# The last two result blocks of a decode layer: other widths, one summed in the bank of the chunks, and their copies and stores on other engines

## The chip, the cores and the metric

The kernel runs on one core of one Trainium2 chip. The metric is the time of one execution on the device in microseconds, the median of several runs. All data are fp32.

## The reference

One transformer layer is computed for eight sequences with one new token each (model width 1024).

```
h   = x + attention(layernorm(x))      # 32 query heads, 4 key/value heads of 128,
                                       # the last 1024 of 4096 cached positions
g   = layernorm(h) @ w_gate            # 1024 x 3584
u   = layernorm(h) @ w_up              # 1024 x 3584
out = h + (gelu(g) * u) @ w_down       # 3584 x 1024
```

The 3584 rows of `w_down` are 28 chunks of 128 rows. The result `out` is a sum over the 28 chunks plus `h`.

## The kernel before, in words

Each weight and each cached key or value is used once per run for only eight tokens. The host lays all of them out as one list of parts in the order of use, and SyncE issues one DMA for each part into two large buffers (`wbuf`). A part is issued when TensorE has finished with the buffer's former content. Most of TensorE's work stands in a loop over stages: eight transposes, then four groups of sixteen products with 512 columns each.

The change lies behind that loop, in the last part of `decode_block`. Chunks 0 to 23 of `w_down` are done in the loop; their sum, with `h`, is gathered by VectorE in `d0`. The activations for all chunks stand transposed in `at`. The 1024 result columns are computed as four groups (NQ = 4) of QW = 256 columns, group j in partitions 32j to 32j + 31, so "column" below means one of these 256.

Chunks 24 to 26 come in parts of two chunks and one (`wd0`, `wd1`), and the function `add` adds their products, and `d0`, in one PSUM bank, `acc`, over 256 columns. ScalarE copies that sum to `s_sb` in SBUF (line 462).

The last chunk, 27, is cut by column into two parts, `we0` and `we1`, whose widths stand in `ENDS`. For each of them TensorE computes four products into a bank of its own (`yt` and `tp`, line 468), VectorE adds `s_sb` and writes `o_fin` (line 471), and the block is stored by a DMA: the first from SyncE's queue, the second from ScalarE's (line 83 is the helper that issues them). SyncE then clears the semaphores and waits for both stores.

The order on each engine is the order of the code. `run` gives each instruction waits on counters of other engines; each engine increments one counter. Where an instruction needs two waits, the first stands as an instruction of its own in front of it. The four products of a block carry their waits on the first of them.

Of the kernel before, what the change touches and what calls it, by code (L numbers as in the profile page):

```python
# [8 lines left out]
P = 128  # L9
# [7 lines left out]
NQ = 4  # L17
CP = 32 // B
QW = D // NQ
# [7 lines left out]
LATE = (5, 6, 4)  # L27

PARTS = (8, 8, 4, 4, 2, 1)
ENDS = (160, 96)  # L30
SINGLES_AT, LAST = 24, 27


class Flow:
# [38 lines left out]
    def run(self, engine, make, *waits, mark=True):  # L73
        ins = self.start(engine, make, waits)
        if not mark:
            return None
        self.done[engine] += 1
        ins.then_inc(self.own[engine], 1)
        return self.own[engine], self.done[engine]

    def move(self, name, out, src, *waits, engine="sync"):
        s = self.sem(name)
        self.start(engine, lambda e: e.dma_start(out, src), waits).then_inc(s, 16)  # L83
        return s, 16
# [6 lines left out]
def decode_block(nc, x, flow, tail, outs):  # L91

    fl = Flow(nc)
    run, move, go = fl.run, fl.move, fl.go
    scale = DH ** -0.5

    def sb(name, *shape):
        return nc.alloc_sbuf_tensor(name, list(shape), F32).ap()

    def bank(name, n):  # L100
        return nc.alloc_psum_tensor(name, [P, n], F32).ap()
# [4 lines left out]
    tp, yt, acc = bank("tp", 2 * N), bank("yt", N), bank("acc", N)  # L106
# [12 lines left out]
    def pe(it, step):  # L119
        return steps, 6 * it + 1 + ("t0", "a0", "a1", "t1", "b0", "b1").index(step)  # L120
# [61 lines left out]
    def load(k, *waits):  # L182
# [15 lines left out]
        out=ident, in_=ident, compare_op=ALU.not_equal, fill=1.0, base=0,  # L198
# [9 lines left out]
        out=own, in_=ident.rearrange("p (a b h) -> p b a h", b=HB, h=REP), axis=AX.XY,  # L208
# [5 lines left out]
    def layernorm(src, ready_, name):  # L214

        bn = sb(name + "_bn", 64, 2, 6)
        mv, ve, sd, r0, r1, r2, rs = (
            sb(f"{name}_{n}", 64, k) for n, k in
            (("mv", 2), ("ve", 1), ("sd", 1), ("r0", 1), ("r1", 1), ("r2", 1), ("rs", 1))
        )  # L220
        a = run("vector", lambda e: e.bn_stats(bn[:, 0], src), ready_)
        run("vector", lambda e: e.tensor_copy(bn[0:32, 1], bn[32:64, 0]), a)
        tok = run("vector", lambda e: e.tensor_copy(bn[32:64, 1], bn[0:32, 0]), a)
        tok = run("vector", lambda e: e.bn_aggr(mv, bn), tok)
        tok = run("vector", lambda e: e.tensor_scalar(ve, mv[:, 1:2], EPS, None, op0=ALU.add), tok)
        tok = run("scalar", lambda e: e.activation(sd, ve, AF.Sqrt), tok)  # L226
        tok = run("vector", lambda e: e.reciprocal(r0, sd), tok)
        tok = run("vector", lambda e: e.scalar_tensor_tensor(
            r1, r0, r0, ve, op0=ALU.mult, op1=ALU.mult), tok)
        tok = run("vector", lambda e: e.tensor_scalar(  # L230
            r2, r1, -0.5, 1.5, op0=ALU.mult, op1=ALU.add), tok)
        tok = run("vector", lambda e: e.tensor_mul(rs, r0, r2), tok)
        return run("vector", lambda e: e.tensor_scalar(
            tin[0:64, 0:N], src, mv[:, 0:1], rs, op0=ALU.subtract, op1=ALU.mult), tok, tin_zero)
# [26 lines left out]
    tok = layernorm(xh, x_in, "ln1")  # L261
# [3 lines left out]
    for hf in range(2):  # L265
# [4 lines left out]
        tok = run("scalar", lambda e: e.copy(q_sb, w0), pe(0, ("a0", "b0")[hf]))  # L270
        tok = run("vector", lambda e: e.tensor_add(tin[:, 0:N], w1, q_sb), tok, pe(0, end),  # L271
                  pe(0, ("t0", "t1")[hf]))
        go("vector", turn, 1, tok, *tp_free)
        qt = tp[:, 0:N].rearrange("p (i s k m) -> p s m k i", i=4, s=2, k=2)
        for s in range(2):
            tok = run("vector", lambda e, s=s: e.tensor_scalar(  # L276
                qz[hf].rearrange("p (s b m) -> p s b m", s=2, b=B)[:, s, :, 0:REP].rearrange(
                    "p b (k i) -> p b k i", k=2),
                qt[:, s, 0::CP], scale, None, op0=ALU.mult), moved, zero[hf])
# [8 lines left out]
    for hf in range(2):  # L288
# [4 lines left out]
        tok = run("vector", lambda e: e.tensor_reduce(  # L293
            out=nmax, in_=s_ps, axis=AX.X, op=ALU.max, negate=True), pe(1, ("a1", "b1")[hf]))
# [3 lines left out]
        tok = run("vector", lambda e: e.reciprocal(rtot, tot), p_ok)  # L298
# [15 lines left out]
    for hf in range(2):  # L314
# [3 lines left out]
        tok = run("scalar", lambda e: e.copy(o1, big[hf][:, 0:N]), pe(2, ("a0", "b0")[hf]))  # L318
        tok = run("vector", lambda e: e.tensor_add(o_sb, big[hf][:, N:2 * N], o1), tok,  # L319
                  pe(2, ("a1", "b1")[hf]))  # L320
        o3 = o_sb.rearrange("p (b d) -> p b d", b=HB)
        out = tin[:, 0:DH]
        tok = run("vector", lambda e: e.tensor_scalar(
            out, o3[:, 0], share[:, 0:1], None, op0=ALU.mult), tok, share_ok,
            pe(2, ("t0", "t1")[hf]))
        for b in range(1, HB):
            tok = run("vector", lambda e: e.scalar_tensor_tensor(
                out, o3[:, b], share[:, b:b + 1], out, op0=ALU.mult, op1=ALU.add), tok)
# [3 lines left out]
        for s in range(2):  # L332
            src = tp[:, 64 * s:64 * s + 64].rearrange("p (b h) -> p h b", h=REP)
            tok = run("vector", lambda e: e.tensor_copy(  # L334
                ot[:, s * REP:(s + 1) * REP], src.unsqueeze(3).to_broadcast([P, REP, B, CP])),
                moved)
# [10 lines left out]
    tok = run("scalar", lambda e: e.copy(y0, ya[:, 0]), pe(3, "a0"))  # L347
    a_out = run("vector", lambda e: e.tensor_add(y1, ya[:, 1], y0), tok, pe(3, "a1"))  # L348
    tok = run("vector", lambda e: e.tensor_add(y1[0:64], y1[0:64], xh), a_out)
# [3 lines left out]
    tok = run("vector", lambda e: e.tensor_add(lo, lo, hi), u, v)  # L353
    top = sb("top", 64, N)
    v = run("scalar", lambda e: e.copy(top, yb[64:P, 1]), pe(3, "b1"))
    tok = run("vector", lambda e: e.tensor_add(lo, yb[0:64, 1], lo), tok, pe(3, "b1"))
# [4 lines left out]
    tok = layernorm(h_sb, h_ok, "ln2")  # L361
    go("vector", turn, 1, tok, pe(3, "t1"))
    xt, tok = spread("xt2", pe(4, "t0"), pe(3, "b1"))
    go("vector", turn, 1, tok)

    at = sb("at", P, DF // P, 32)
# [5 lines left out]
    tok = run("scalar", lambda e: e.copy(gs[0], ya[:, 0]), pe(4, "a0"))  # L372
    tok = run("vector", lambda e: e.tensor_add(gs[0], ya[:, 1], gs[0]), tok, pe(4, "a1"))
    go("vector", ready[0], 3, tok)
    g_ok = run("scalar", lambda e: e.activation(ge[0], gs[0], AF.Gelu_apprx_tanh), tok)
    tok = run("vector", lambda e: e.tensor_copy(us[0], yb[:, 0]), pe(4, "b0"))  # L376
    tok = run("vector", lambda e: e.tensor_add(us[0], yb[:, 1], us[0]), tok, pe(4, "b1"))  # L377
    b_free = tok
    tok = run("vector", lambda e: e.tensor_mul(tin[:, 0:N], ge[0], us[0]), tok, g_ok, pe(4, "t1"))
# [24 lines left out]
    tok = run("scalar", lambda e: e.copy(gs[1], ya[:, 0]), pe(5, "a0"))  # L404
    tok = run("vector", lambda e: e.tensor_add(gs[1], ya[:, 1], gs[1]), tok, pe(5, "a1"))  # L405
# [6 lines left out]
    tok = run("vector", lambda e: e.tensor_add(us[1][0:64], yb[0:64, 0], top), v)  # L412
    tok = run("vector", lambda e: e.tensor_mul(tin[0:64, 0:N], ge[1][0:64], us[1][0:64]), tok)  # L413
# [11 lines left out]
    q0, place = SINGLES_AT, 0  # L425
    for k, src in enumerate(tail[:-len(ENDS)]):
        n = src.shape[1] // D
        here = move(f"wd{k}", later[:, place:place + n * D], src, pe(5, "b0"))
# [3 lines left out]
    blocks = []  # L432
    c0 = 0
    for k, (n, src) in enumerate(zip(ENDS, tail[-len(ENDS):])):
        w = later[:, place + NQ * c0:place + NQ * (c0 + n)]
# [4 lines left out]
    tok = run("scalar", lambda e: e.copy(d0, yb[:, 1]), pe(5, "b1"))  # L440
    tok = run("vector", lambda e: e.tensor_add(d0[0:64], d0[0:64], h_sb), tok)
    for k in range(2):
        tok = run("vector", lambda e: e.tensor_add(d0, ya[:, k], d0), tok, pe(6, f"a{k}"))  # L443
# [3 lines left out]
    def add(lhs, rhs, *waits, start=False, stop=False):  # L447
        for j in range(NQ):
            tok = run("tensor", lambda e: e.matmul(
                acc[32 * j:32 * j + 32, 0:QW], lhs(j), rhs(j), start=start, stop=stop),  # L450
                *waits, mark=(stop and j == NQ - 1))
        return tok

    for q in range(SINGLES_AT, LAST):
        if q == LAST - 1:
            add(lambda j: add2[:, j // 2, :], lambda j: d0[:, (j % 2) * QW:(j % 2) * QW + QW],
                d_ok, consts)
        w, here = rows[q]
        tok = add(lambda j: at[:, q, :], lambda j: w[:, j * QW:(j + 1) * QW], here, at_ok[1],
                  start=(q == SINGLES_AT), stop=(q == LAST - 1))  # L460
    s_sb = sb("s_sb", P, QW)
    s_ok = run("scalar", lambda e: e.copy(s_sb, acc[:, 0:QW]), tok)
    o_fin = sb("o_fin", P, QW)
    done = []
    cut = ENDS[0]
    for (c0, n, w, here), d_ps in zip(blocks, (yt, tp)):
        for j in range(NQ):
            tok = run("tensor", lambda e: e.matmul(  # L468
                d_ps[32 * j:32 * j + 32, 0:n], at[:, LAST, :], w[:, j * n:(j + 1) * n],
                start=True, stop=True), here, mark=(j == NQ - 1))  # L470
        done.append(run("vector", lambda e: e.tensor_add(  # L471
            o_fin[:, c0:c0 + n], d_ps[:, 0:n], s_sb[:, c0:c0 + n]), tok, s_ok))

    nc.vector.br_lt(never, 0, on_true="down", on_false="end").branch_hint(back)
    nc.switch_bb("end")
    sent = [move("out0", outs[0], o_fin[:, 0:cut], done[0]),
            move("out1", outs[1], o_fin[:, cut:QW], done[1], engine="scalar")]

    issued = fl.sem("issued")
    nc.scalar.sem_inc(issued, 1)  # L480
# [75 lines left out]
```

## Time and profile before

| | us |
|---|---|
| median of 3 runs (lowest, highest) | 264.25 (264.11, 264.62) |
| the profiled execution, its own time | 264.19 |
| its span, first to last instruction | 262.8 |
| share of the span in which the weights' queue is busy | 98.4% |

The profile is one execution. Times in its rows count from the start of the span. PE is TensorE's products, PEld its weight loads, DVE VectorE, ACT ScalarE, SP SyncE; SPq and ACTq are the issue of a DMA by these engines. A row of the timeline gives the start, the length, the engine, the line, the operation with output and input, the count, and in brackets the idle time before it and what ended that. An fp32 product stands as two records, so a group of four products is "x8". [...]

### The profile page before, as it was taken

The page shows a single profiled execution, that of the slowest core. Times are in us where ns is not written, and L with a number is a line of the kernel's source. Part 1 is how long each engine was busy: PE and PEld are TensorE (multiplying, and loading weights), DVE is VectorE, ACT ScalarE, POOL GpSimd, SP SyncE. Part 2 cuts the span into 40 slices and gives each one's busy share as a digit, 9 for nine tenths or more (in the row PEclk, how much of TensorE's full clock was granted, in tenths as well). Part 3 has the DMA queues.
Part 4 walks back from the last instruction along what each step waited for, and adds up shares of the span by engine and source line. Part 5 has one row for each costly group of instructions (what it writes and reads, how often), then busy time and mean ns, then how long its engine had stood idle before and what let it go on. Part 6 is the DMA issues. An engine that isn't in the chain of part 4 may idle for free. (4 is left out here: it accounts for less than half of the span.)

```text
span 262.8 us, 2313 instructions
## 1 busy us (share of the span) xinstructions
PE 157.1 (60%) x984; PEld 53.1 (20%) x984; DVE 34.5 (13%) x78; ACT 16.6 (6%) x25; POOL 15.8 (6%) x31
## 2 busy tenths in 40 slices
PE   0024955915937726947617918629909609968596
PEld 0021221211221222212102212122302202323122
DVE  0220010010021110040310020640100300031011
ACT  1000000000030020000000000200200000010000
POOL 5020010010000000001020000020000110000100
PEclk9999996895975955986965995956986965997799
DMA  8998997999899799989979997998999799999995
GB/s 319 484 409 389 479 469 329 479 479 449 349 479 479 329 469 479 449 349 479 479 329 469 479 459 339 479 479 359 439 479 459 339 449 429 414 454 409 429 415 213
DMA packets 3200, 111.31 MB, mean 424 GB/s; under 512 B 496, under 2 KB 752, under 8 KB 1024
## 3 DMA queue, kind: packets, MB, share of 16 engines
q1 hardware_dynamic: 3024, 111.23, 98.4%
q10 hardware_dynamic: 176, 0.08, 0.1%
HBM read 111.18 MB, written 0.13 MB: 424 GB/s over the span
## 5 line engine op out<-in xcount | busy, mean ns | idle before, releaser
L146 PE MATMUL big<-w,st 128*32 128x512 f32 x832 | 137.2, 747 | 68.7 <-PEq L127 67.1
L146 PEld LDWEIGHTS big<-w,st 128*32 128x32 f32 x832 | 37.8, 133 | 160.1 <-issue 157.5
L132 PE MATMUL tp<-ident,tin 128*128 128x128 f32 x104 | 17.5, 322 | 34.4 <-PEq L127 34.4
L132 PEld LDWEIGHTS tp<-ident,tin 128*128 128x128 f32 x104 | 14.0, 166 | 44.7 <-issue 44.7
L255 POOL COPY st<-ot 128x256 f32<-128x256 f32 x8 | 2.9, 401 | 75.4 <-DVE ot L334 75.4
L246 POOL COPY st<-xt 128x1024 f32<-128x1024 f32 x2 | 3.0, 1523 | 54.1 <-DVE xt L241 54.1
L293 DVE TENSOR_REDUCE nmax<-big 128x1 f32<-128x1024 f32 x2 | 2.5, 1225 | 29.0 <-PE big L146 29.0
L271 DVE TENSOR_TENSOR tin<-big,q 128x512 f32<-128x512 f32 x2 | 1.4, 692 | 32.7 <-PE big L146 32.7
L319 DVE TENSOR_TENSOR o<-big,o 128x512 f32<-128x512 f32 x2 | 1.4, 692 | 28.6 <-PE big L146 28.6
L281 POOL COPY st<-qz 128x1280 f32<-128x1280 f32 x2 | 2.5, 1254 | 35.5 <-DVE qz L276 35.5
L255 POOL COPY st<-at 128x256 f32<-128x256 f32 x6 | 2.6, 465 | 32.7 <-DVE tin L413 25.1
L270 ACT COPY q<-big 128x512 f32<-128x512 f32 x2 | 1.2, 586 | 36.0 <-PE big L146 36.0
L405 DVE TENSOR_TENSOR gs<-big,gs 128x512 f32<-128x512 f32 x1 | 0.7, 691 | 19.1 <-PE big L146 19.1
L443 DVE TENSOR_TENSOR d<-big,d 128x512 f32<-128x512 f32 x2 | 1.4, 692 | 13.2 <-PE big L146 13.2
L348 DVE TENSOR_TENSOR y<-big,y 128x512 f32<-128x512 f32 x1 | 0.7, 692 | 18.4 <-PE big L146 18.4
L255 POOL COPY st<-xt 128x256 f32<-128x256 f32 x2 | 1.3, 660 | 30.1 <-DVE us L377 30.1
L318 ACT COPY o<-big 128x512 f32<-128x512 f32 x2 | 1.2, 585 | 28.9 <-PE big L146 28.9
L295 ACT ACTIVATE tin<-big,nmax 128x1024 f32<-128x1024 f32 x2 | 2.2, 1114 | 11.9 <-DVE nmax L293 11.9
L295 ACT ACT_TABLE_LOAD x1 | 1.3, 1283 | 25.1 <-DVE nmax L293 25.1
L226 ACT ACT_TABLE_LOAD x2 | 2.6, 1283 | 1.9 <-POOL ident L197 1.9
L404 ACT COPY gs<-big 128x512 f32<-128x512 f32 x1 | 0.6, 585 | 32.3 <-PE big L146 32.3
L376 DVE COPY us<-big 128x512 f32<-128x512 f32 x1 | 0.7, 692 | 13.1 <-PE big L146 13.1
(69 smaller groups left out, 42.2 us busy)
## 6 DMA issues: line engine op xcount, KB each, us to landing
w<-weights SPq DMA_DIRECT2D x3, 4096.0 KB, 22.3
w<-weights SPq DMA_DIRECT2D x2, 2048.0 KB, 23.3
w<-weights SPq DMA_DIRECT2D x1, 1024.0 KB, 23.8
w<-weights SPq DMA_DIRECT2D x1, 512.0 KB, 24.8
w<-weights SPq DMA_DIRECT2D x1, 320.0 KB, 25.1
w<-weights SPq DMA_DIRECT2D x1, 192.0 KB, 25.1
w<-weights SPq DMA_DIRECT2D x11, 26.9
out<-o_fin SPq DMA_DIRECT2D x1, 80.0 KB, 1.7
```

The lines of the kernel that those rows point to most:

```text
L132: ins = t.transpose(tp[:, i * P:(i + 1) * P], tin[:, i * P:(i + 1) * P], ident)
L146: ins = t.matmul(out[32 * j:32 * j + 32, :], st[i][:, s0:s0 + 32], wbuf[i][:, w0:w0 + N], start=(c == 0), stop=(c == 3))
L226: tok = run("scalar", lambda e: e.activation(sd, ve, AF.Sqrt), tok)
L246: fill = run(engine, lambda e: e.tensor_copy(windows(i), half.unsqueeze(2).to_broadcast([P, 2, NQ, 4 * 32])), tok, *clear)
L255: tok = run(engine, lambda e: e.tensor_copy(windows(i)[:, k, 2 * e2:2 * e2 + 2].rearrange("p h (c m) -> p h c m", m=32), s[:, e2].unsqueez ...
L270: tok = run("scalar", lambda e: e.copy(q_sb, w0), pe(0, ("a0", "b0")[hf]))
L271: tok = run("vector", lambda e: e.tensor_add(tin[:, 0:N], w1, q_sb), tok, pe(0, end), pe(0, ("t0", "t1")[hf]))
L281: fill = run("gpsimd", lambda e: e.tensor_copy(st[hf].rearrange("p (k n) -> p k n", k=2), qz[hf].unsqueeze(1).to_broadcast([P, 2, NQ * WIN ...
L293: tok = run("vector", lambda e: e.tensor_reduce(out=nmax, in_=s_ps, axis=AX.X, op=ALU.max, negate=True), pe(1, ("a1", "b1")[hf]))
L295: p_ok = run("scalar", lambda e: e.activation(tin, s_ps, AF.Exp, bias=nmax, accum_out=tot), tok, pe(1, ("t0", "t1")[hf]))
L319: tok = run("vector", lambda e: e.tensor_add(o_sb, big[hf][:, N:2 * N], o1), tok, pe(2, ("a1", "b1")[hf]))
L443: tok = run("vector", lambda e: e.tensor_add(d0, ya[:, k], d0), tok, pe(6, f"a{k}"))
```

## The change

The blocks are 176 and 80 columns wide. The first is no longer computed in a bank of its own: its products are added in `acc`, on top of the chunks' sum, and ScalarE copies the 176 finished columns straight to `o_fin` and stores them from its own queue. Before that VectorE copies the other 80 columns of the sum out of `acc` to `s_sb`, and the first block's products wait for this copy besides their weights. The second block has the bank `yt`, VectorE's addition, and a store from SyncE's queue.

```diff
-ENDS = (160, 96)
+ENDS = (176, 80)
...
-    s_sb = sb("s_sb", P, QW)
-    s_ok = run("scalar", lambda e: e.copy(s_sb, acc[:, 0:QW]), tok)
+    (a0, na, wa, a_here), (b0, nb, wb, b_here) = blocks
+    cut = na
+    s_sb = sb("s_sb", P, nb)
+    s_ok = run("vector", lambda e: e.tensor_copy(s_sb, acc[:, b0:b0 + nb]), tok)
     o_fin = sb("o_fin", P, QW)
-    done = []
-    cut = ENDS[0]
-    for (c0, n, w, here), d_ps in zip(blocks, (yt, tp)):
+
+    def last(out, n, w, start, *waits):
         for j in range(NQ):
             tok = run("tensor", lambda e: e.matmul(
-                d_ps[32 * j:32 * j + 32, 0:n], at[:, LAST, :], w[:, j * n:(j + 1) * n],
-                start=True, stop=True), here, mark=(j == NQ - 1))
-        done.append(run("vector", lambda e: e.tensor_add(
-            o_fin[:, c0:c0 + n], d_ps[:, 0:n], s_sb[:, c0:c0 + n]), tok, s_ok))
+                out[32 * j:32 * j + 32, 0:n], at[:, LAST, :], w[:, j * n:(j + 1) * n],
+                start=start, stop=True, skip_group_check=not start), *waits, mark=(j == NQ - 1))
+        return tok
+
+    done = [run("scalar", lambda e: e.copy(o_fin[:, 0:na], acc[:, 0:na]),
+                last(acc, na, wa, False, s_ok, a_here))]
+    done.append(run("vector", lambda e: e.tensor_add(o_fin[:, b0:b0 + nb], yt[:, 0:nb], s_sb),
+                    last(yt, nb, wb, True, b_here)))
...
-    sent = [move("out0", outs[0], o_fin[:, 0:cut], done[0]),
-            move("out1", outs[1], o_fin[:, cut:QW], done[1], engine="scalar")]
+    sent = [move("out0", outs[0], o_fin[:, 0:cut], done[0], engine="scalar"),
+            move("out1", outs[1], o_fin[:, cut:QW], done[1])]
```

On TensorE, at the end of its program, the order of the products changes as follows (lines with - stand in the kernel before, with + in the changed one; in brackets the counters that an instruction waits for, `wd1`, `we0` and `we1` being the landings of the last three weight parts):

```order
 L449 MATMUL acc<-w,at 32x256 [waits wd1_done]
 L449 MATMUL acc<-w,at 32x256 x3
-L468 MATMUL yt<-w,at 32x160 [waits we0_done]
-L468 MATMUL yt<-w,at 32x160 x3
-L468 MATMUL tp<-w,at 32x96 [waits we1_done]
-L468 MATMUL tp<-w,at 32x96 x3
+L470 MATMUL acc<-w,at 32x176 [waits vector_done,we0_done]
+L470 MATMUL acc<-w,at 32x176 x3
+L470 MATMUL yt<-w,at 32x80 [waits we1_done]
+L470 MATMUL yt<-w,at 32x80 x3
```

The first block's products stand where they stood, write `acc`, and have a wait for VectorE in front of the one for their weights.

On VectorE, at the end of its program, the two additions become a copy and an addition:

```order
 L441 TENSOR_TENSOR d<-d,h_sb 64x512 [waits scalar_done]
 L443 TENSOR_TENSOR d<-big,d 128x512 [waits vector_done,steps_done] x2
-L471 TENSOR_TENSOR o_fin<-yt,s_sb 128x160 [waits tensor_done,scalar_done]
-L471 TENSOR_TENSOR o_fin<-tp,s_sb 128x96 [waits tensor_done]
-L474 COMPARE_AND_BRANCH
+L465 COPY s_sb<-acc 128x80 [waits tensor_done]
+L477 TENSOR_TENSOR o_fin<-yt,s_sb 128x80 [waits tensor_done]
+L480 COMPARE_AND_BRANCH
```

The copy of the sum moved here from ScalarE, and only the second block's addition is left.

On ScalarE, also at the end, the copy and the store are those of the first block:

```order
 L411 COPY top<-big 64x512 [waits steps_done]
 L440 COPY d<-big 128x512 [waits steps_done]
-L462 COPY s_sb<-acc 128x256 [waits tensor_done]
-L83 DMA out<-o_fin 128x96 [waits vector_done]
+L475 COPY o_fin<-acc 128x176 [waits tensor_done]
+L83 DMA out<-o_fin 128x176 [waits scalar_done]
```

The store waits for ScalarE's own copy in place of VectorE's addition.

## Rows read from the trace of the kernel before

**Rows 1.** The page: span, queue share, bytes and mean rate
```profile
span 262.8 us, 2313 instructions
DMA packets 3200, 111.31 MB, mean 424 GB/s; under 512 B 496, under 2 KB 752, under 8 KB 1024
q1 hardware_dynamic: 3024, 111.23, 98.4%
```

**Rows 2.** The chain that ended last, around the end: start, length, what
```profile
234.86 25.11 DMA w<-weights
```

**Rows 3.** The timeline at the end: start, length, engine, line, operation, count, idle before
```profile
257.99 1.07 PE L449 MATMUL acc<-w,at 128*32 128x256 f32 x16 [0.52 <-DMA w<-weights]
259.28 0.64 PE L449 MATMUL acc<-w,at 128*32 128x256 f32 x8
259.98 0.37 ACT L462 COPY s_sb<-acc 128x256 f32<-128x256 f32 x1 [17.93 <-PE acc L449]
260.00 0.48 PE L468 MATMUL yt<-w,at 128*32 128x160 f32 x8
260.46 0.16 PEld L468 LDWEIGHTS tp<-w,at 128*32 128x32 f32 x8 [0.30 <-DMA w<-weights]
260.47 0.37 PE L468 MATMUL tp<-w,at 128*32 128x96 f32 x8
260.62 0.33 DVE L471 TENSOR_TENSOR o_fin<-yt,s_sb 128x160 f32<-128x160 f32 x1 [2.41 <-PE yt L468]
260.91 0.26 DVE L471 TENSOR_TENSOR o_fin<-tp,s_sb 128x96 f32<-128x96 f32 x1
260.98 0.35 SPq L83 DMA_DIRECT2D out<-o_fin  x1
261.20 0.36 ACTq L83 DMA_DIRECT2D out<-o_fin  x1
```

**Rows 4.** SyncE's queue: issue of the last weight transfer (start, length)
```profile
235.33 0.43 SPq L83 DMA_DIRECT2D w<-weights  x1
```

**Rows 5.** DMA issues: source, queue, count, KB of one, us to landing
```profile
w<-weights SPq DMA_DIRECT2D x1, 192.0 KB, 25.1
out<-o_fin SPq DMA_DIRECT2D x1, 80.0 KB, 1.7
out<-o_fin ACTq DMA_DIRECT2D x1, 48.0 KB, 1.6
```

**Rows 6.** Groups by form: line, engine, shapes, count, busy, mean ns of one
```profile
L334 DVE COPY ot<-tp 128x256 f32<-128x256 f32 x4 | 1.5, 420 | 2.6 <-PE tp L132 2.6
L241 DVE COPY xt<-tp 128x128 f32<-128x128 f32 x4 | 1.0, 286 | 4.4 <-PE tp L132 4.4
...
L270 ACT COPY q<-big 128x512 f32<-128x512 f32 x2 | 1.2, 586 | 36.0 <-PE big L146 36.0
```

**Rows 7.** The timeline where VectorE's result releases TensorE
```profile
207.57 0.69 DVE L379 TENSOR_TENSOR tin<-ge,us 128x512 f32<-128x512 f32 x1
208.43 0.53 PEld L132 LDWEIGHTS tp<-ident,tin 128*128 128x128 f32 x5 [2.64 <-issue]
```

**Rows 8.** Windows over the stores: length, PE, PEld, DVE, ACT, POOL, clock, DMA, GB/s
```profile
261.90:262.00 0.10, 0.00 (x0) 0.00 (x0) 0.00 (x0) 0.00 (x0) 0.00 (x0) 1.00 1.01 298
262.30:262.40 0.10, 0.00 (x0) 0.00 (x0) 0.00 (x0) 0.00 (x0) 0.00 (x0) 1.00 0.44 112
```

**Rows 9.** Tile w from 233 us: count, shortest, median, longest ns
```profile
L146 PE MATMUL big<-w,st x108: 589/592/1061, 232.5 to 256.9; 128*32 128x512 f32 x108
```

**Rows 10.** Windows over two quiet stretches of TensorE, as in rows 8
```profile
257.46:257.99 0.53, 0.01 (x2) 0.03 (x2) 0.47 (x1) 0.00 (x0) 0.00 (x0) 1.00 1.04 417
...
210.00:212.00 2.00, 0.00 (x0) 0.00 (x0) 0.25 (x1) 0.00 (x0) 0.74 (x2) 1.00 1.21 524
212.00:213.00 1.00, 0.00 (x0) 0.00 (x0) 0.00 (x0) 0.00 (x0) 0.00 (x0) 0.60 0.61 262
```

## The prediction

> **What bounds the kernel now.** I read the page first. The queue that carries the weights is busy for 98.4% of the 262.8 us and moves 424 GB/s on average [rows 1], so all but the last microseconds are a stream of weights that the change does not touch. What it can change is the tail behind the last weights, so I next read the chain that ended last. It goes through the transfer of the first result block, which is issued at 234.86 and lands 25.11 us later, at 259.97 [rows 2]; TensorE's products for it start at 260.00 [rows 3].
>
> In the timeline of the tail I then looked at the second block, because the chain shows only one of the two. Its weights are issued at 235.33 [rows 4] and take 25.1 us [rows 5], so they land at about 260.43. TensorE's first load for it starts at 260.46 after an idle time put down to that transfer [rows 3]. So each block waits for its own weights, the blocks are 0.46 us apart, and VectorE's second addition starts at 260.91, which is 0.07 after its products end (260.47 + 0.37 = 260.84), not behind the first addition (260.62 + 0.33 = 260.95). The ends are a store issued at 260.98 that lands 1.7 us later and one issued at 261.20 that lands 1.6 us later, at 262.80 [rows 3, 5], the end of the span.
>
> The reader should also see what lies beside the path: ScalarE copies the finished sum out of the bank of all chunks from 259.98 to 260.35 while TensorE already works in another bank from 260.00 [rows 3]. That copy costs nothing now, since it is done before the first addition.
>
> **The change, step by step.** All times are on the clock of the profiled execution.
>
> *The new wait.* The last products of the chunks end at 259.28 + 0.64 = 259.92, and ScalarE's copy begins 0.06 later [rows 3]. VectorE's copy of 80 columns should begin at the same 259.98. Its price: VectorE's copies out of such a bank take 420 ns for 256 columns and 286 for 128 [rows 6], 1.05 ns per column, so 80 columns take 286 - 50 = 236 ns. It ends at 260.22. TensorE's next group now waits for it, with everything behind it on that engine: both blocks' products.
>
> From that copy to TensorE there is no such hop in the trace with one result and one load on either side. The nearest short row is a transfer that lands at 259.97 and lets TensorE go at 260.00, 0.03 [rows 2, 3]. The nearest long one is VectorE's product that ends at 208.26 and releases a load at 208.43, 0.17 [rows 7], but there VectorE and TensorE each spend another semaphore instruction. What a second wait in front of an instruction costs can be seen on VectorE: its addition with two waits starts 0.14 after the products (260.48 to 260.62), the one with one wait 0.07 after. I take 0.03 + 0.07 = 0.10, keep 0.03 and 0.17 as bounds, and TensorE starts at 260.32.
>
> [...]
>
> *The weights.* The first block's transfer grows by 16 of 256 columns, 32 KB, at 424 GB/s 0.08 us [rows 1]: 260.05 instead of 259.97. This lies under the new wait. The last byte of both blocks is where it was, so 260.43 stays for the second.
>
> *First block.* Eight products take 0.48 at 160 columns and 0.37 at 96 [rows 3], 1.7 ns per column, so 0.51 at 176: to 260.83. ScalarE starts 0.06 later, at 260.89. Its copy takes 0.37 us at 256 columns [rows 3] and 586 ns at 512 [rows 6], 0.84 ns per column, so 0.30 at 176, to 261.19. The addition of VectorE is gone from this block. The store is issued by the same engine; from an addition to its store it was 0.03 (261.17 to 261.20) [rows 3], so the first store goes out at 261.22, 0.24 later than the 260.98 of before. Behind it on ScalarE stands one semaphore increment; behind the other store, now on SyncE's queue, stand the clearing of semaphores and the wait for both stores, all of it under the 1.6 us of landing.
>
> *Second block.* Two groups of 256 columns take 1.07 where one takes 0.64 [rows 3], so a group follows 0.43 behind the one before it; for 176 columns that is 0.43 x 176/256 = 0.30. It starts at 260.62 and takes 0.37 - 0.03 = 0.34 at 80 columns, to 260.96 (in strict sequence it would be 260.83 + 0.34 = 261.17, the upper bound). VectorE starts 0.07 later and takes 0.24 (0.26 at 96 columns, less 16 columns), to 261.27, and the store goes out at 261.30, 0.10 later than 261.20.
>
> *The stores.* If each landed as before for itself, they would land at 261.22 + 1.7 = 262.92 and 261.30 + 1.6 = 262.90, against 262.80: +0.12. But the two were 0.22 apart and are now 0.08 apart, with 128 KB in all as before, and the DMA engines are full at 261.90 and still at 0.44 at 262.35 [rows 8]: the stores' bytes already ran as one piece. Then the end follows the first store's issue, +0.24. The full engines speak for the second reading, so I take +0.20, two thirds of the way.
>
> **Sum.** 264.19 + 0.20 = 264.39 for the profiled execution; the median of the runs is 0.06 above it, so 264.45. Lower bound: hop 0.03 (-0.07) and stores that land independently, +0.05: 264.30. Upper bound: hop 0.17 and the blocks in strict sequence, 260.39 + 0.51 + 0.34 + 0.07 + 0.24 + 0.03 = 261.58, and 1.7 to land: 263.28, +0.48: 264.73.
>
> **Rivals.** *TensorE's clock falls in the new pause (ends slower).* TensorE stands still from 259.92 to 260.32. [...] It decides if the clock falls before 260.32. Against it: a pause of 0.53 at 257.46 left the clock at 1.00, and with no product at all from 210 to 212 it was still 1.00 and fell only in the next microsecond, to a mean of 0.60 [rows 10].
>
> *The wait is hidden (not slower).* If VectorE's copy and the hop were done by 260.05, when the first block's weights land, TensorE would start at 260.08, the second block would again wait only for 260.43, and its 16 columns fewer would save 0.03 in the products and 0.02 in the addition: 264.20. The copy would have to be done 0.27 earlier; for it speaks only that the ends of products are modelled, against it that ScalarE's start at 259.98 is a recorded one [rows 3].
>
> *The upper bounds come together.* The groups on TensorE do not overlap and the stores run as one piece behind the later issue: +0.48, up to 264.8. For it: the blocks now use one engine's sequencer with more waits. Against it: two groups in 1.07 [rows 3].
>
> **How the numbers follow.** 0.2% of this time, 0.53 us, is about what a measurement can tell from no change. The forecast has 0.75, the hidden wait 0.13, the upper bounds 0.07, the clock 0.05. The forecast's bounds (264.30 to 264.73) lie within 0.2%; I give 0.04 of its 0.75 to slower and 0.01 to faster for the spread of the runs (264.11 to 264.62). Of the hidden wait 0.03 is faster, of the upper bounds 0.05 and of the clock 0.04 slower. Together: faster 0.04, same 0.83, slower 0.13. The range leaves out the clock and reaches from just under the hidden wait, 264.1, to just over the upper bounds, 264.85.
>
> **What would show it.** VectorE's copy of about 0.24 us from about 259.98; TensorE idle from 259.92 to about 260.32 and released by that copy, not by a transfer; ScalarE's copy of 0.30 ending near 261.19 with its store right behind; the second addition ending near 261.27; the stores' issues closer than 0.22, and the span near 263.0. I am wrong if TensorE's first load of the first block still follows its transfer, if the granted clock is below 1.00 in the tail, if the stores land in under 1.5 us, or if the span moves for a reason that lies before 257 us.

## The result and the profile after

The changed kernel takes 264.59 us (median of 22 runs, 264.3 to 265.55), the kernel before 264.17 (22 runs, 263.98 to 264.64). The ratio is 1.0019 with a 95% interval of 1.0013 to 1.0025: slower by 0.42 us by the medians and by 0.50 (0.34 to 0.66) by the ratio. That is more than twice the 0.20 that the sum gave; the median still lies inside the forecast's bounds, 264.30 to 264.73.

The profiled execution took 264.69. The timeline of its tail (start, length, engine, line, operation, count, idle before):

```profile
259.41 0.64 PE L449 MATMUL acc<-w,at 128*32 128x256 f32 x8
260.11 0.24 DVE L465 COPY s_sb<-acc 128x80 f32<-128x80 f32 x1 [1.77 <-PE acc L449]
260.47 0.19 PEld L470 LDWEIGHTS acc<-w,at 128*32 128x32 f32 x8 [0.90 <-DMA w<-weights]
260.50 0.51 PE L470 MATMUL acc<-w,at 128*32 128x176 f32 x8 [0.45 <-DVE s_sb L465]
260.65 0.30 PEld L470 LDWEIGHTS yt<-w,at 128*32 128x32 f32 x8
260.80 0.35 PE L470 MATMUL yt<-w,at 128*32 128x80 f32 x8
261.06 0.30 ACT L475 COPY o_fin<-acc 128x176 f32<-128x176 f32 x1 [20.59 <-PE acc L470]
261.20 0.24 DVE L477 TENSOR_TENSOR o_fin<-yt,s_sb 128x80 f32<-128x80 f32 x1 [0.85 <-PE yt L470]
261.40 0.39 ACTq L83 DMA_DIRECT2D out<-o_fin  x1
261.47 0.35 SPq L83 DMA_DIRECT2D out<-o_fin  x1
```

The weights came 0.13 later in this execution (chunk 26's products start at 259.41, before at 259.28 [rows 3]), so the tails are compared from that start. The first block's products follow it by 1.09 (before 0.72), the first store by 1.99 (before 1.70), the second by 2.06 (before 1.92). In the fourth row the pause is named: TensorE stands idle for 0.45, ended by VectorE's copy. The row above it, the weight load, still names the transfer, which is the wait that stands on the load itself. But the transfer was over: issued at 234.89 and 25.3 us under way, it has its last landing in the trace at 260.18, 0.29 before the load, and in the pause the DMA engines move next to nothing (window below). The chain that ended last (start, length, what) runs through the copy too:

```profile
260.11 0.25 DVE s_sb L465
260.37 0.14 issue
260.50 0.51 PE acc L470 x8
```

The stores in the list of DMA issues (KB, us to landing):

```profile
out<-o_fin ACTq DMA_DIRECT2D x1, 88.0 KB, 1.8
out<-o_fin SPq DMA_DIRECT2D x1, 40.0 KB, 1.9
```

Both land later after their issue than before (1.7 and 1.6 [rows 5]). To two digits the landings in the traces give 1.66 and 1.60 before, 1.77 and 1.86 now. From the first store's issue to the last landing it is 1.82 before and 1.93 now, and from the start of chunk 26's products to the last landing 3.52 before and 3.92 now. I call this last time the tail; its 0.40 more is the 0.29 of the first store's issue and 0.11 in the landings. Windows over the stores, over the pause and over TensorE's last products (columns as in [rows 8]):

```profile
262.40:262.50 0.10, 0.00 (x0) 0.00 (x0) 0.00 (x0) 0.00 (x0) 0.00 (x0) 1.00 1.06 345
262.70:262.80 0.10, 0.00 (x0) 0.00 (x0) 0.00 (x0) 0.00 (x0) 0.00 (x0) 1.00 0.73 159
262.80:262.90 0.10, 0.00 (x0) 0.00 (x0) 0.00 (x0) 0.00 (x0) 0.00 (x0) 1.00 0.08 16
...
260.00:260.50 0.50, 0.06 (x4) 0.03 (x1) 0.24 (x1) 0.00 (x0) 0.00 (x0) 1.00 0.01 3
260.50:261.20 0.70, 0.65 (x16) 0.46 (x16) 0.00 (x0) 0.14 (x1) 0.00 (x0) 1.00 0.00 0
```

The DMA engines are full with the stores at 262.4 (share 1.06), and TensorE's granted clock is 1.00, full speed, in the pause and behind it.

### The profile page after: what moved, and what is told of

It reads as the page before. It is cut to its first block, busy times and chain, and to the rows that moved or that the text cites. A ratio compares the mean times of both kernels' runs of the same rounds, so it can differ in the third digit from the quotient of the medians.

```text
span 263.4 us, 2313 instructions
## 1 busy us (share of the span) xinstructions
PE 154.8 (59%) x984; PEld 52.7 (20%) x984; DVE 34.5 (13%) x78; ACT 16.5 (6%) x25; POOL 15.8 (6%) x31
## 2 busy tenths in 40 slices
DMA packets 3200, 111.31 MB, mean 423 GB/s; under 512 B 496, under 2 KB 752, under 8 KB 1024
## 5 line engine op out<-in xcount | busy, mean ns | idle before, releaser
L146 PE MATMUL big<-w,st 128*32 128x512 f32 x832 | 135.1, 736 | 71.1 <-PEq L127 69.3
L146 PEld LDWEIGHTS big<-w,st 128*32 128x32 f32 x832 | 37.2, 132 | 160.9 <-issue 158.4
## 6 DMA issues: line engine op xcount, KB each, us to landing
w<-weights SPq DMA_DIRECT2D x1, 352.0 KB, 25.3
```

Source lines behind the costliest of these rows:

```text
L146: ins = t.matmul(out[32 * j:32 * j + 32, :], st[i][:, s0:s0 + 32], wbuf[i][:, w0:w0 + N], start=(c == 0), stop=(c == 3))
```

## The experiments

**Theory**: TensorE's products for the first block, which add in the bank `acc`, wait for VectorE's copy out of it (0.45 idle), and the stores' bytes then run as one piece behind the later first store. **Rivals**: the widths, ScalarE's copy and store, or the exchange of the stores' queues cost the time.

**e1, widths alone.**

```diff
-ENDS = (160, 96)
+ENDS = (176, 80)
```

> The kernel before with the widths 176 and 80 alone: two banks, two additions on VectorE, stores as before. First theory (the pause for VectorE's copy, with the stores' bytes running as one piece behind the first store, makes the change slower): no pause here, the first block's store goes out about 0.1 us later (0.08 for its longer transfer, 0.03 for longer products), the second about 0.05 earlier, so 0 to +0.1 us against the kernel before. Rival (the widths themselves cost it: a longer first transfer, rows of 320 bytes in the second store): +0.3 us or more.

264.30, ratio 1.0003 (0.9994 to 1.0012), which is +0.08 us between -0.16 and +0.32. Its timeline:

```profile
259.47 0.64 PE L449 MATMUL acc<-w,at 128*32 128x256 f32 x8
...
260.66 0.35 PE L468 MATMUL tp<-w,at 128*32 128x80 f32 x8
260.92 0.34 DVE L471 TENSOR_TENSOR o_fin<-yt,s_sb 128x176 f32<-128x176 f32 x1 [2.51 <-PE yt L468]
261.18 0.23 DVE L471 TENSOR_TENSOR o_fin<-tp,s_sb 128x80 f32<-128x80 f32 x1
261.29 0.35 SPq L83 DMA_DIRECT2D out<-o_fin  x1
261.44 0.36 ACTq L83 DMA_DIRECT2D out<-o_fin  x1
```

The widths alone don't explain the change, but they may cost a part of it: counted from chunk 26's products, the first store goes out 0.12 later than before (1.82) and the second 0.05 later (1.97), and the tail is 3.66 against 3.52. The second was expected 0.05 earlier. That was a miss: its addition starts 0.17 after its products end (261.01), where it was 0.07 before, and follows the longer first addition.

**e2, the roles exchanged.**

```diff
-ENDS = (176, 80)
+ENDS = (160, 96)
...
+    done = [run("vector", lambda e: e.tensor_add(o_fin[:, b0:b0 + nb], yt[:, 0:nb], s_sb),
+                last(yt, nb, wb, True, b_here), s_ok)]
+    done.append(run("scalar", lambda e: e.copy(o_fin[:, a0:a0 + na], acc[:, a0:a0 + na]),
+                    last(acc[:, a0:a0 + na], na, wa, False, s_ok, a_here)))
...
```

> The changed kernel with the blocks' roles exchanged and the old widths: the first block (160) has the bank of its own, VectorE's addition and SyncE's store, the second (96) adds in the bank of the chunks and ScalarE copies and stores it. The copy that TensorE waits for (now 160 columns, 0.33 us, done near 260.31) then lies under the landing of the second block's weights at 260.43. First theory: -0.05 to +0.05 us against the kernel before. Rival (adding in the bank of the chunks, or ScalarE's copy and store, costs time by itself): +0.2 us or more.

264.32, ratio 1.0004 (0.9995 to 1.0013, at most +0.34 us): not told from the kernel before. Its timeline:

```profile
260.06 0.33 DVE L465 COPY s_sb<-acc 128x160 f32<-128x160 f32 x1 [1.76 <-PE acc L449]
...
260.57 0.16 PEld L470 LDWEIGHTS acc<-w,at 128*32 128x32 f32 x8 [0.31 <-DMA w<-weights]
```

The copy is done at 260.39, and TensorE goes on at 260.57 with the transfer; with the 0.15 that the changed kernel has behind its copy it would be 260.54, so the copy is hidden by little. The tail is 3.49, before 3.52. Adding in `acc` and ScalarE's copy and store are there as in the changed kernel, and cost nothing that can be measured.

**e3, the copy twice.**

```diff
+    again = sb("again", P, nb)
+    s_ok = run("vector", lambda e: e.tensor_copy(again, acc[:, b0:b0 + nb]), tok)
```

> The changed kernel with VectorE's copy of the 80 columns made twice, and TensorE waiting for the second one. First theory: what lengthens the copy lengthens the run one to one; the second copy follows 0.15 to 0.24 us behind the first, so +0.57 to +0.66 us against the kernel before (+0.15 to +0.24 against the changed kernel). Rival (the pause is not on the path that ends last): the same as the changed kernel, +0.42.

264.74, ratio 1.0019 (1.0010 to 1.0028). By the medians that is 0.58 above the kernel before, where the changed kernel has 0.42; by the ratio it is the same as the changed kernel, so the times of the runs don't show a difference between the two. The trace does:

```profile
260.00 0.24 DVE L465 COPY s_sb<-acc 128x80 f32<-128x80 f32 x1 [1.75 <-PE acc L449]
260.16 0.23 DVE L467 COPY again<-acc 128x80 f32<-128x80 f32 x1
...
260.53 0.51 PE L472 MATMUL acc<-w,at 128*32 128x176 f32 x8 [0.59 <-DVE again L467]
```

The pause grew from 0.45 to 0.59 and the tail from 3.92 to 4.10 in the one execution that was profiled, as the theory has it.

**e4, no pause, by a second bank.** Each chunk's products, and those of `d0`, are made in two pieces.

```diff
+            for out, a, n in ((acc, 0, ENDS[0]), (tp, ENDS[0], ENDS[1])):
...
-    s_ok = run("vector", lambda e: e.tensor_copy(s_sb, acc[:, b0:b0 + nb]), tok)
+    s_ok = run("vector", lambda e: e.tensor_copy(s_sb, tp[:, 0:nb]), tok)
...
-                last(acc, na, wa, False, s_ok, a_here))]
+                last(acc, na, wa, False, a_here))]
...
```

> The changed kernel, but the chunks' sum for the last 80 columns stands in another bank (each chunk's products are made in two pieces, 176 and 80 columns), so VectorE's copy reads another bank than the one in which the first block adds, and TensorE doesn't wait for it. First theory: the first block starts with its weights at about 260.09, its store goes out at 260.99, the second at 261.14: -0.1 to +0.1 us against the kernel before. Rival (the longer first transfer, ScalarE's copy and store, or the small second store cost the time): +0.3 us or more, as in the changed kernel.

266.92, ratio 1.0102 (1.0088 to 1.0116): a miss for every theory. TensorE stops in the middle of the first block:

```profile
260.25 0.50 PE L471 MATMUL acc<-w,at 128*32 128x176 f32 x6
...
262.89 0.34 PE L471 MATMUL acc<-w,at 128*32 128x176 f32 x1 [2.14 <-issue]
```

"issue" means that it waited for nothing that the profile shows. The kernel has 40 products in this tail instead of 24, and e4 says nothing about the pause.

**e11, as many products, one bank.** The kernel before, with 40 products.

```diff
+        for a, n in ((0, 176), (176, 80)):
+            for j in range(NQ):
+                tok = run("tensor", lambda e: e.matmul(
+                    acc[32 * j:32 * j + 32, a:a + n], lhs(j), rhs(j)[:, a:a + n],
...
```

> The kernel before with each chunk's products of the tail made in two pieces (176 and 80 columns) in the one bank that they have: 40 products in TensorE's tail where it has 24. e4, which has the same 40 and a second bank, lost 2 us while TensorE waited for nothing that the profile shows. If the number of products (the length of the program) is the cause: +2 to +3 us here too, with an idle stretch of that kind in the last products. If the second bank is the cause: within 0.2 us of the kernel before.

267.40, ratio 1.0118 (1.0102 to 1.0133). The gap stands at the same place, behind six of the eight records of the first block:

```profile
260.13 0.47 PE L470 MATMUL yt<-w,at 128*32 128x160 f32 x6
...
263.13 0.37 PE L470 MATMUL yt<-w,at 128*32 128x160 f32 x1 [2.53 <-issue]
```

So the second bank is not its cause. What e4 and e11 share is the sixteen products more; why they stop TensorE no run shows.

**e5 and e6, the pair with few products.** Both leave out the products of chunk 25 and of `d0`. e5 has the two pieces, the second bank and no pause, as e4, and 24 products; e6 has the pause. The edit that both share:

```diff
-    for q in range(SINGLES_AT, LAST):
-        if q == LAST - 1:
-            add(lambda j: add2[:, j // 2, :], lambda j: d0[:, (j % 2) * QW:(j % 2) * QW + QW],
-                d_ok, consts)
+    for q in (SINGLES_AT, LAST - 1):
```

> As e4, but with as many products on TensorE's tail as the changed kernel has (24): the products for chunk 25 and those for the gathered sum of chunks 0 to 23 are left out, so that part of the result is missing; all transfers stay. Chunks 24 and 26 are made in two pieces, the copy reads another bank, TensorE doesn't wait for it. First theory: the first block starts with its weights, no stall of 2 us, -0.1 to +0.1 us against the kernel before, and about 0.4 less than e6. Rival (without the pause the changed kernel is as slow, since the longer first transfer or ScalarE's copy and store cost it): +0.3 us or more.

> The changed kernel with the same products left out as in e5 (chunk 25 and the gathered sum of chunks 0 to 23, so part of the result is missing), with the pause as it is. First theory: the left-out products lay under transfers, so +0.3 to +0.5 us against the kernel before, as the changed kernel. Rival (e5 gains by the left-out work and not by the pause): as e5.

e5: 264.08, ratio 0.9997 (0.9989 to 1.0006). e6: 264.49, ratio 1.0009 (1.0001 to 1.0018). They stood beside each other on one chip and differ by 0.41 us by the medians and 0.32 by the ratios. The timeline of e5 and its stores in the list of DMA issues:

```profile
259.81 0.24 DVE L463 COPY s_sb<-tp 128x80 f32<-128x80 f32 x1 [1.67 <-PE tp L450]
259.99 0.16 PEld L468 LDWEIGHTS acc<-w,at 128*32 128x32 f32 x8 [0.44 <-DMA w<-weights]
259.99 0.51 PE L468 MATMUL acc<-w,at 128*32 128x176 f32 x8 [0.26 <-DMA w<-weights]
...
260.90 0.36 ACTq L83 DMA_DIRECT2D out<-o_fin  x1
261.12 0.35 SPq L83 DMA_DIRECT2D out<-o_fin  x1
...
out<-o_fin ACTq DMA_DIRECT2D x1, 88.0 KB, 1.7
out<-o_fin SPq DMA_DIRECT2D x1, 40.0 KB, 1.6
```

TensorE starts under the running copy, which reads another bank, and waits only for the transfer. Widths, ScalarE's copy and both stores are those of the changed kernel. The pause, with all that follows from it, is worth 0.3 to 0.4 us: the tails are 3.62 in e5 and 3.93 in e6, 0.31 apart. e5's tail is 0.10 longer than that of the kernel before; its first products start 0.89 after those of chunk 26, released by the transfer, where it was 0.72 before. In the changed kernel this later transfer lies under the pause.

**e8, the second store alone.** The first block's 176 columns are not stored.

```diff
-    sent = [move("out0", outs[0], o_fin[:, 0:cut], done[0], engine="scalar"),
-            move("out1", outs[1], o_fin[:, cut:QW], done[1])]
+    sent = [move("out1", outs[1], o_fin[:, cut:QW], done[1])]
...
+    nc.scalar.wait_ge(*done[0])
     nc.scalar.sem_inc(issued, 1)
```

> The changed kernel without the first block's store (its 176 columns aren't written). First theory: the second store's landing was late because its bytes run behind the first's on the same DMA engines; alone it lands within 1.60 us of its issue or less, where it took 1.86, so the run is 0.2 to 0.3 us shorter than the changed kernel. Rival (a store of rows of 320 bytes from SyncE takes 1.8 us by itself): the landing stays at 1.8 or more and the time at +0.42.

264.26, ratio 1.0008 (0.9999 to 1.0017), 0.33 less than the changed kernel by the medians; the tail is 3.58 against 3.92.

```profile
out<-o_fin SPq DMA_DIRECT2D x1, 40.0 KB, 1.5
```

The same store lands 0.34 sooner after its issue (1.52 against 1.86) when no other runs in front of it. Issued 0.07 behind the first, it ends where the two together end.

**e7, e9 and e10, the queues.** e7 and e10 are one kernel, e9 is the changed kernel.

```diff
-    sent = [move("out0", outs[0], o_fin[:, 0:cut], done[0], engine="scalar"),
-            move("out1", outs[1], o_fin[:, cut:QW], done[1])]
+    sent = [move("out0", outs[0], o_fin[:, 0:cut], done[0]),
+            move("out1", outs[1], o_fin[:, cut:QW], done[1], engine="scalar")]
```

> The changed kernel with the stores' queues as before: the first block's store from SyncE, the second's from ScalarE. First theory: the stores run as one piece behind the first issue; that issue has one hop from ScalarE to SyncE instead of none, so the same as the changed kernel within 0.1 us, +0.3 to +0.5 against the kernel before. Rival (the queues' exchange costs it): +0.1 or less against the kernel before.

> The changed kernel once more, beside e10 on the same chip. +0.35 to +0.5 us against the kernel before; stores issued 0.07 apart that land 1.8 and 1.9 us after their issue.

> e7 once more (the stores' queues as before), beside e9. In the trace of e7 the stores landed 1.6 and 1.7 us after their issue, 0.2 less than in the changed kernel, but its weights came later and the run was no shorter. If the queues matter: the same short landings and 0.1 to 0.2 us less than e9. If they don't: as e9, with landings of 1.8 and 1.9.

e7: 264.70, ratio 1.0017 (1.0008 to 1.0027). e9: 264.56, 1.0013 (1.0004 to 1.0023). e10: 264.55, 1.0013 (1.0001 to 1.0025). The rival had +0.1 us or less for e7; its interval starts at +0.21, so the queues' exchange is not what costs the 0.4. The landings do differ, in both traces; e10:

```profile
261.52 0.35 SPq L83 DMA_DIRECT2D out<-o_fin  x1
261.60 0.36 ACTq L83 DMA_DIRECT2D out<-o_fin  x1
...
out<-o_fin SPq DMA_DIRECT2D x1, 88.0 KB, 1.6
out<-o_fin ACTq DMA_DIRECT2D x1, 40.0 KB, 1.7
```

against 1.8 and 1.9 in e9. From the first issue to the last landing it is 1.80 and 1.81 in e7 and e10, and 1.96 in e9; the tail is 3.78 in both, and 3.95 in e9. The medians of e9 and e10 are 0.01 apart, but each ratio is known to about 0.3 us only, so they neither show a gain of 0.15 nor exclude it.

## Why the prediction was right, and where its size was off

**The pause: right.** VectorE's copy starts 0.70 after chunk 26's products, as ScalarE's did, and takes the 0.24 of the forecast. From its end (260.35) to the products it is 0.15, where I took 0.10 between bounds of 0.03 and 0.17. I had started from the 0.03 of a transfer; from an engine's result to another engine [rows 3] have 0.06 and 0.07, and with the 0.07 for a second wait that would have been nearer. The first block's weights land under the pause: their last landing is at 260.18, and e5, which doesn't wait for the copy, starts its products 0.89 after chunk 26's where the changed kernel has 1.09. e5 against e6 gives the price of the pause with all that follows from it, 0.3 to 0.4.

**What the wait rests on.** The wait is the program's. That the products may not begin while the copy still reads their bank was the author's assumption, and no run shows it: the kernel without the wait in one bank was not tried. In e5 the copy reads another bank and nothing waits for it; the products start at 259.99 while it runs (259.81 to 260.05).

**The blocks: right.** 0.51 for the first group, 0.30 from it to the second, 0.35 for that (0.34), 0.30 for ScalarE's copy, 0.24 for the addition. The first store goes out 0.29 later than before, from chunk 26's products on, where the sum has 0.24; the 0.05 is the hop. The second goes out 0.14 later, forecast 0.10.

**The stores: the term that was too small.** I weighed stores that land each for itself (+0.12) against stores that run as one piece (+0.24) and took +0.20. The second reading is the better one. In the eight traces of before, e1, e2, e4, e5, e7, e10 and e11 the stores are issued 0.08 to 0.22 apart, and the last landing comes 1.78 to 1.84 after the first issue in all of them; and the second store alone, in e8, lands after 1.52. With the measured hop that is +0.29. The other 0.11 of the tail is a term that I put at nothing: in the changed kernel, e3, e6 and e9 the last landing comes 1.93 to 1.96 after the first issue. ScalarE's queue in front is not enough for it, since e4 and e5 have the same queues and 1.82. The four differ from these two in that SyncE's store follows 0.07 behind ScalarE's, where e4 and e5 have 0.14 and 0.22, and ScalarE's issue takes 0.39 and not 0.36. Why the landing is then later is not shown.

**The rivals.** The clock stayed at 1.00 through the pause. What a lower one costs, the trace of before shows elsewhere: from 237 to 239 us the granted clock is 0.50, and products of 512 columns that start there take 1024 to 1061 ns, where the median is 592 [rows 9]. The hidden wait is not this kernel, but e2 and e5 build it, and neither can be told from the kernel before. The blocks do overlap on TensorE (the second starts 0.30 after the first, which takes 0.51), so the upper bounds did not come together. That the measured +0.42 still lies below their +0.48 is luck in part: the bound had its room from a strict sequence that did not happen, and the time went into the hop and the landings. The gain that could have paid for the pause is not there: the addition that the first block lost (0.33) has a copy of nearly the same length in its place (0.30), and the copy that ScalarE lost lay beside TensorE's products (from 259.98 and from 260.00 [rows 3]).

## What to carry to other kernels

Before a product is added on top of a sum in a bank, look who still reads that bank: a copy of other columns in it, for which the program makes the product wait, held TensorE up here for its whole length and the hop behind it (0.24 and 0.15), and the work that this saves may have been free. Give that bank to the block whose data come last, as e2 does, and the wait lies under the transfer (there the copy was done at 260.39, and TensorE went on with the transfer at 260.57). Two stores issued close together ended as one here, 128 KB 1.78 to 1.96 us behind the first issue; price such a pair by the first issue and not each by its own landing.

## What was not expected of the hardware

Sixteen more products in the straight part of TensorE's program behind its loop stop it for 2.1 to 2.5 us at one place of the program (e4, e11), at +2.8 and +3.2 us in the medians, while it waits for nothing that the profile shows. e5, in two pieces and two banks too but with 24 products, has no such gap. What holds TensorE in the gap no run shows.
